# A retention layer and a two-step mixer on one core: the hand-written order of all work is searched anew

## The chip, the cores and the metric

The kernel runs on one core of a Trainium2 chip. Time is the device time of one execution in microseconds (us); lower is better. The kernel before takes 189.88 us, the median of three runs (189.71 to 190.01).

## The reference

For 4 batches, 8 heads, 768 positions and a head size of 64, a retention layer runs over the positions with a decaying state, and its result goes through a mixer that first mixes the 768 positions (through 256) and then the 512 channels (through 1536):

```python
gamma = 1.0 - 2.0 ** (-5.0 - np.arange(H))          # one decay per head
for t in range(S):                                   # retention
    state = gamma * state + k[:, :, t] (outer) v[:, :, t]
    y[:, :, t] = q[:, :, t] @ state / sqrt(D)
x = y, heads side by side: (4, 768, 512)
h  = relu(x.T @ w_tok1) @ w_tok2                     # 768 -> 256 -> 768
u  = x + h.T
out = u + relu(u @ w_ch1) @ w_ch2                    # 512 -> 1536 -> 512
```

## The kernel before

**Work.** There are 16 units for the first half, one for each batch (0 to 3) and pair of heads (0 to 3). A unit loads q, k and v of its two heads (768 positions in six chunks of 128). k is scaled by a decay (L343 on ACT, L345 on DVE) and transposed into `kT` (on PE, L379, and copied out of PSUM, L392; or by a DMA transpose on SP, L367). q is transposed into `qT` (PE, L377, then L387 on DVE with the decay; or L367). PE forms the state of each chunk (L408), DVE adds these up chunk by chunk (`U`, L418 and L420), and the sums are scaled into `diag` (L434 on ACT, L436 on DVE). PE forms the scores inside a chunk (L453), DVE masks them (`am`, L463), PE multiplies them with v (L474) and adds the part of the older chunks (L483). Then follow the two products of the position mixer (L503 with `wt1`, L523 with `wt2`) with a rectifier between (L512, L514), casts to 16 bits (L489, L529), a copy into `X` (L539) and a transpose into `uT` (PE, L568 and L575; or a DMA transpose on SP, L553).

The second half is done batch by batch: `widen` (512 to 1536 channels; L606 and L622 for batches 0 and 1, and a form with seven instead of eight products for batches 2 and 3, L647 to L717) and `narrow` (1536 to 512; L784 to L862, and L746 and L755 for the last five row blocks), with the stores to `out`.

**Loads.** Batches 0 and 1 are loaded by POOL with a cast to 16 bits (k, v and q of a pair are slabs of 192 KB each), between them the weights. k of the first pair, and all of batches 2 and 3, are requested by SP without a cast.

**The order.** Each piece of work is an `Op` with the engine it may run on. The string `PLAN` (L40) is the order in which all of them are written out, with the engine and the PSUM bank of each: two digits for an Op, one for the engine where it has a choice, one for each bank. Each engine executes its own instructions in the order in which they were written, and waits where an operand is not there. A `+` and a digit in `PLAN` stand for that many *zero products* (L935): products of a tile of zeros into bank 7 which nobody reads. The Ops' `deps`, costs and `dma` figures are what the search for `PLAN` works with; the program that is built depends on `PLAN` alone (`placed`, L70), and its waits follow from the tiles that are read and written.

Of the kernel before, what the change touches and what calls it, by code (L numbers as in the profile page):

```python
# [39 lines left out]
PLAN = (  # L40
    "0b04000a0903010d05020c060f1h11i107+h1j00e1W11k0081X0h+41l01m0g+81w011v230k1z+21n41A2x50i1y1o1p0j1S01T11q1r0m"
    "+91U31s1x1V00p+21Y42y1B226312706292t01Z2b2u020211t00l+9386221u02v1390n+11C1E51F1D0282z61G0230r2w02A2a2B0u241"
    "+72I102c42C2502L+11H31I2M2f12g1J02D2d2Q02E2e0+12H362h02K+11K2F01N2J1L02i62G11O00q2j2N31M11Q72k02O1P00E2l3412P0"
    "2o3512R0o2m01R13652p03710w2S03a72T62n03b2U0t3c2q03d3j452V03i123e0s3n2W3f4k62X03k3L70x3g03l2Z3h03m2r13003o23H1"
    "3p3r43103I13s2Y13253q03J03M3t03u33303v3K15s73w04l3N52s03x3A3y05taC10z3B0aF63C03z13D70y3F3E13V24303G1aD3OaG3Y0v"
    "bf7aE3XbgaHbc13P0Fbd4g14h1aL63Qbe3RaMbh0A4i43SaN3WaI14j00Dbl5bm0CaJ404bn4u2673aK0Bb353T04xbi13U03Z0Gbjb974P1bk"
    "4wba4304Q1444yb0641b44v4204R3b5b1451bb4T2b24m54V74S04n4614o474UbA6480b634pbB4qbJ24WbC4r494XbK4s1b74a1bL4cb8"
    "5326514b0aU3574d0aV1d4faR4aWaO15o14e055aP4t0aX34Y0I5p1aY4z60H4AaZaS56aQ0Kbu04ZaTbx30N504C1544D510bybM4B0bG7bv"
    "bObHbwbNbr24E0bs521bz4F019bIbo44G15bpbD7bqbE165q3602bQ45r04H118bS50MbFbt4I174L58259cc7bR15a0c84J05b35ccd14K0"
    "bX0bP5d0bVc94M04N05Y15e6cabW05f5Z0bZ5g162061cb5u6630651ch66c00bY0L675k5v68c44O5w5x5h5yc5c15i05z64bT5l0cj6ci1"  # L50
    "5m069cl5j0ck0Oc2cA2cm06acu6y05C10356z0cwcq5G6C00JcF45F6b05ncB5A0cy55D5B0cncr6B6D05E7806d7123cG5H0cz06ecJ6E790"
    "cv5I5K7cK5L5J0cD6f6A25M06h5N4cE05O6c10QcH6g5P00R7a05QcI10P5T5R0cx6i20W6j5U06l4co6m7b5V05S17f36F66k05W1cpce05X0"
    "6G6HcM6I6n06Jdn16Kdocfde66L1cQ07gcNcR1adF7cSdf7h7c0dq57idrdg7jdG7kds7d16o6dH6p7edz56q1dA7M16N6730dB7N10S6r6P7O"
    "cW56s06QcXdb76OcYdc6R7I0cZ3d0c37J06u6t06M1dR07Ldd6S51ed52dp6TcLd67K26U06V111dS1fd16Wd7dh76v17l0di6X1dO28S08T1"
    "6Y36w0dP8V6ZdTd24dQ701d80djcgd90V7m0bU716xcCda7n73267217P07qd3730740T7pcs0dk5d40U751dldC47Q7odmcT37RcU7rdDcV7S"
    "e671bdE77760e0e43e77X1465e1e508m0dX7e3dYe9818n1dw57Tea00Xdxe2dZ7s2a317ta20ed8k27U7Ydy0YdI07ZdJ12dU180dKdV8o8j1"
    "8i0dt61cdL0dW1gdM7V08l821dudN8U2eb4ee07u07v0dv7weO57x0eI7y6eJ7zeieL7A07W0eP7Bec7Ee883855ej8408p6eK86ef8708q8r"
    "7C0es38s7D0em8877F0eo898W07Heq2eg8X0eheT48a07G013et8ber0eU8YeM08c0en8d08e8tepeN0eX8f0eu8g0eR8u8heY8v08x45619w0"
    "eS18Z38A9x010ex7908w0c618zeV0Z918Bct1eveW0eycO1c7092f0cP18yew09y93ezf1949s1970415eA09508F399148GeE9t0f49608C4"
    "989v8DeB8E09b8H0f80eQ9c59a8I6f9a42eC8Jf59f19g8K0fm79u2eZ9d8L9e0eFfa6fnfceH1fb8M0fo29h08Of79i6fdfp9j8P1ff9k0fq"  # L60
    "eD8Rfg9z68N0a92f69ofraa9l8Q0aba5fe49A9m0acfkfh9n0ftfs39Bfuf21adfiae9p0fD5fv9q0fy9Cgm2fE9DfF1fz9EfHfjflfwfGfI"
    "9H4076gnfxfR1a609JfKfSfJ3fAfLfT09KfV9F0fMfP9G0fUgqfWga79LfNa70fYfOgrgo6a8g80fCgpgtg9ge3fBfZfX6gbfQgc9Ig3gugs5"
    "gAgdgyg4gvgfgz9P1g09Qgggwg6g1ghgkg59M29NglgBgi9O0h34gZ9R0g29S0af09Tgjh40gH6gx9U0h19Vah5037h09W09Yag0g7alh89Z0"
    "gCa00ha7a1ak9X0ajgJ1ek0gDh90gI09rap0aih52gEaqam5h2hch6anhbgMao0gGhd0hegKar0h7eG0hhgLgN1as1hlatgFgQau0el0hfhp1"
    "hmgR0hgavhq0gO7aw0hnax0ayhihr2hoaz0gPaA0huaBhshtgVhv0hk0hj1gSgWgY1hw2gThHhL6hygUhxig7hz0hJi10hMhZ4hIihhAhKhN5"
    "hBhPhCii3hQikhOhDhF1ilf31i0hR5hEgX0hSijhG1inhTi3ioim3hUi4iL1ipi52i6i2hVhXi7hWiu0ibi8iZ5idici9ieiviqiahYiw4iyir"
    "j0iN6ixiMisizj3iPj4j14iBj2j6iCiR3iOiQiA4jdj7iGiDiSitj56iHiJjY7iTj8iEifjbiUj9jciXjek60jaiYk7jZiIjCk0k1jEk2iFiV"
    "iKk8iWk9kak3jfjDjk3jFkbjl0jG4jgk4jI1jH0jijN6k51jLjOjhjr7jM0kcjRjjjJjPjsjSjpjKjQ0jTjUjq0jtjW1jVkd1jX0jvju0ke4jw"
    "jm6jxjyjnjA1kfjokgkhjzkikjjB0kkkl0"
)  # L70


# [24 lines left out]
def kernel(  # L97
# [171 lines left out]
    def load(b, p, what):  # L269
        src = dict(k=k, q=q, v=v)[what][b, 2 * p:2 * p + 2]  # L270
        hard = (b, p, what) in HARD
        plain = b in PLAIN
        wide = what == "q" and TURN[b, p, "q"] == "w"
        inner = what == "k" and not hard and not plain
        s = Slot("us" if hard else "v" if what == "v" and not plain else "row")
        if inner:
            s = pairs[b, p]

        def emit():
            if plain:  # L280
                t = tile_of(s, [P, 2, NC, D], FP)
                nc.sync.dma_start(out=t, in_=src.rearrange("h (c p) d -> p h c d", p=P))
                return
            if hard:
                t = tile_of(s, [P, 3, N2], FP)
                t = s.tile = t.rearrange("p a b -> p (a b)").rearrange("p (h c d) -> p h c d", h=2, c=NC)
            elif what == "v":
                t = tile_of(s, [P, 2, NC, D], F16)
            else:
                t = (s.tile if inner else tile_of(s, [P, 2, 2, NC, D], F16))[:, int(inner)]  # L290
            if wide:
                nc.gpsimd.dma_start(out=t.rearrange("p h c d -> p h (c d)"),
                                    in_=src.rearrange("h (p c) d -> p h (c d)", c=NC))
            else:
                (nc.sync if hard else nc.gpsimd).dma_start(out=t, in_=src.rearrange("h (c p) d -> p h c d", p=P))
# [672 lines left out]
```

## Time and profile before

| | |
|---|---|
| median of 3 runs | 189.88 us (189.71 to 190.01) |
| the profiled execution | 189.72 us |
| its span, from the first to the last instruction | 187.9 us |
| PE busy | 182.2 us (97%) |
| DVE busy | 163.0 us (87%) |
| ACT busy | 126.2 us (67%) |
| zero products (L935) | 62, busy 14.8 us |

PE, DVE, ACT, POOL and SP are the engines; PEld is the weight load of PE. A row such as `L935 PE MATMUL bank<-zero ... x62 | 14.8, 382` names the line, the engine, the operation, its tiles, how many there are, the time in which at least one of them was running, and the mean duration of one in ns. Products overlap on PE, so that the busy time divided by the count is less than the mean. Between 189.72 us and the span lie 1.8 us outside the first and the last instruction.

### The profile page before, as it was taken

What the parts mean: (1) busy time and instruction counts of PE and PEld (TensorE: products, weight loads), DVE (VectorE), ACT (ScalarE), POOL (GpSimd) and SP (SyncE); (2) the same over time, 40 slices, a digit from 0 to 9 for tenths busy, and PEclk for the clock granted to TensorE, in tenths of its full rate; (3) what the DMA queues carried; (4) which work ended last, traced back from release to release, by engine and by line L of the source; (5) the groups of instructions that cost most, each with busy time, mean ns of one, the idle gap of its engine ahead of it and who ended that gap; (6) DMA issues with size and microseconds to landing.
All of it is one profiled execution on the core that took longest, in us unless ns stands there. A gap on an engine that the chain in (4) does not pass through costs nothing.

```text
span 187.9 us, 5270 instructions
## 1 busy us (share of the span) xinstructions
PE 182.2 (97%) x2102; PEld 137.5 (73%) x2102; DVE 163.0 (87%) x424; ACT 126.2 (67%) x288; POOL 36.2 (19%) x45
## 2 busy tenths in 40 slices
PE   7999999999999999999999999999999999999993
PEld 3556789667679879767677988875589986656882
DVE  3789899978799998989896999999999988879973
ACT  7227789677868697579868696899975535682220
POOL 8992659520020001000103100210000000000000
PEclk9999999999999999999999999999999999999999
DMA  6999999999999799999999999998206464500133
GB/s 101 168 165 196 175 178 187 172 187 207 187 211 221 153 116 222 193 203 205 194 244 161 220 149 221 349 161 214 42 0 108 147 65 176 197 0 5 56 140 140
DMA packets 94233, 30.23 MB, mean 161 GB/s; under 512 B 84352, under 2 KB 91264, under 8 KB 94208
## 3 DMA queue, kind: packets, MB, share of 16 engines
q1 hardware_dynamic: 62560, 18.95, 56.1%
q0 software_dynamic: 30208, 8.46, 44.0%
q10 hardware_dynamic: 1440, 2.49, 4.5%
q8 instruction: 16, 0.26, 0.6%
q14 instruction: 9, 0.07, 0.2%
HBM read 26.74 MB, written 6.29 MB: 176 GB/s over the span
## 4 chain that ended last, share of the span: by engine, by line
PE 82%; DMA 5%; ACT 5%; DVE 4%; issue 1%; DVEq 0%; ACTq 0%
PE bank L606 14%; PE bank L820 13%; PE bank L679 12%; PE bank L830 9%; PE bank L935 6%; PE bank L523 6%; PE bank L503 6%; PE bank L453 3%; PE bank L474 3%; DMA qT<-q 3%; PE bank L746 3%; DMA uT<-u 2%; PE bank L483 2%; PE bank L408 2%; PE bank L377 2%; ACT h L622 2%
## 5 line engine op out<-in xcount | busy, mean ns | idle before, releaser
L463 DVE TENSOR_TENSOR am<-bank,mask 128x384 f16<-128x384 f32 x64 | 33.6, 549 | 4.4 <-PE bank L453 4.0
L606 PE MATMUL bank<-uT,wc 128*128 128x384 f16 x192 | 36.0, 326 | 0.0
L622 ACT ACTIVATE h<-bank 128x384 f16<-128x384 f32 x48 | 21.6, 491 | 9.1 <-PE bank L606 7.2
L606 PEld LDWEIGHTS <-wc 128*128 128x128 f16 x192 | 17.4, 98 | 9.1 <-DVE uT L575 0.2
L360 POOL CAST v<-row 128x768 f16<-128x768 f32 x7 | 7.4, 1067 | 76.6 <-DMA row<-in_v_dram 50.4
L696 DVE TENSOR_TENSOR h<-bank,us 128x384 f16<-128x384 f32 x36 | 18.9, 552 | 2.8 <-PE bank L679 1.8
L810 ACT COPY us<-bank 128x256 f32<-128x256 f32 x27 | 10.1, 377 | 15.8 <-PE bank L820 15.6
L820 PEld LDWEIGHTS <-hs 128*128 128x128 f16 x198 | 18.7, 98 | 2.4
L837 DVE TENSOR_TENSOR X<-X,bank 128x256 f32<-128x256 f32 x44 | 17.7, 414 | 2.4 <-PE bank L830 1.5
L691 ACT COPY us<-bank 128x384 f32<-128x384 f32 x36 | 16.3, 490 | 4.3 <-PE bank L679 3.3
L489 ACT CAST x<-bank 128x384 f16<-128x384 f32 x30 | 14.0, 487 | 6.7 <-PE bank L483 6.6
L420 DVE SCALAR_TENSOR_TENSOR U<-U,gp,bank 128x64 f32<-128x64 f32 x64 | 17.4, 275 | 1.0
L820 PE MATMUL bank<-wsum,hs 128*128 128x256 f16 x132 | 17.6, 273 | 0.0
L935 PE MATMUL bank<-zero 128*128 128x384 f16 x62 | 14.8, 382 | 1.1 <-DVE zero L928 1.1
L679 PE MATMUL bank<-hs,wsum 128*128 128x384 f16 x72 | 15.0, 326 | 0.1
L529 ACT CAST u<-bank 128x384 f16<-128x384 f32 x27 | 12.6, 487 | 3.5 <-PE bank L523 3.3
L523 PE MATMUL bank<-h,wt 128*128 128x128 f16 x192 | 14.8, 219 | 0.0
L434 ACT ACTIVATE diag<-U,gp 64x320 f16<-64x320 f32 x25 | 13.8, 558 | 0.4
L679 PEld LDWEIGHTS <-wsum 128*128 128x128 f16 x96 | 9.3, 97 | 6.4 <-issue 0.5
L503 PE MATMUL bank<-x,wt 128*128 128x128 f16 x192 | 13.7, 219 | 0.0
L830 PEld LDWEIGHTS <-h 128*128 128x128 f16 x132 | 12.5, 98 | 1.5
L539 ACT COPY X<-bank 128x384 f32<-128x384 f32 x28 | 13.4, 494 | 0.1
(89 smaller groups left out, 365.8 us busy)
## 6 DMA issues: line engine op xcount, KB each, us to landing
out_dram<-X SPq DMA_DIRECT2D x14, 256.0 KB, 4.3
row<-in_v_dram SPq DMA_DIRECT2D x8, 384.0 KB, 5.5
row<-in_k_dram SPq DMA_DIRECT2D x8, 384.0 KB, 6.0
row<-in_q_dram SPq DMA_DIRECT2D x8, 384.0 KB, 5.5
wc<-in_moe_w_ch_dram POOLq DMA_DIRECT2D x5, 512.0 KB, 12.6
out_dram<-X ACTq DMA_DIRECT2D x9, 256.0 KB, 3.0
row<-in_q_dram POOLq DMA_DIRECT2D x8, 192.0 KB, 6.1
v<-in_v_dram POOLq DMA_DIRECT2D x8, 192.0 KB, 8.4
```

Source lines behind the costliest of these rows:

```text
L420: nc.vector.scalar_tensor_tensor(out=u[:, c], in0=u[:, c - 1], scalar=gp[:, p:p + 1], in1=st, op0=ALU.mult, op1=ALU.add)
L463: nc.vector.tensor_tensor(am, SC[g].tile[:, :m * P].rearrange("p (i t) -> p i t", t=P), mask.to_broadcast([P, m, P]), ALU.mult)
L503: nc.tensor.matmul(acc[:, jt * P:(jt + 1) * P], wt1[:, i, jt * P:(jt + 1) * P], X16.tile[:, i], start=(i + jt == 0), stop=(i == NC - 1), s ...
L523: nc.tensor.matmul(Y[hf].tile[:, i * P:(i + 1) * P], wt2[:, jt, t], H1.tile[:, jt], start=False, stop=(jt == NJ - 1), skip_group_check=True)
L606: nc.tensor.matmul(acc[:, :SH], wc1[:, ct, ft * P:(ft + 1) * P], UT.tile[:, ct, sh * SH:(sh + 1) * SH], start=(ct == 0), stop=(ct == NP - 1))
L622: nc.scalar.activation(H2.tile[:, ft], A.tile[:, :SH], AF.Relu)
L679: nc.tensor.matmul(acc[:, :SH], left(ct), r[:, ct], start=first and ct == 0, stop=ct == 1, skip_group_check=True)
L696: nc.vector.tensor_tensor(into(hf)[:, ft], bank.tile[:, :SH], kept(j), ALU.add)
L820: nc.tensor.matmul(acc_[:, lo], l[:, j], r[:, j], start=first and j == 0, stop=j == K2 - 1, skip_group_check=True)
L830: nc.tensor.matmul(acc_[:, lo], l[:, j], r[:, j], start=first and j == 0, stop=j == K2 - 1, skip_group_check=True)
L837: (nc.vector if e == "DVE" else nc.gpsimd).tensor_tensor(dst(), dst(), b_(), ALU.add)
L935: nc.tensor.matmul(spare[:, :384], zero[:, :P], zero, start=True, stop=True)
```

## The change

`PLAN` is replaced as a whole; the Ops, their instructions and the data they move are the same. In the search's rules one condition is dropped: a request for k no longer waits for the landing of q of the same pair, which shares its tile.

```diff
 PLAN = (
-    "0b04000a0903010d05020c060f1h11i107+h1j00e1W11k0081X0h+41l01m0g+81w011v230k1z+21n41A2x50i1y1o1p0j1S01T11q1r0m"
...
+    "00010b04050703021h0080f061i1+e1n00d1o1p1j11k00a1q1r1s1t0090e1u00c0g+11l2+21W01m0h1X0i0j+11v210k1w341z1S11A0m1x"
...
         elif inner:
-            o = Op(ops, (-20, 0, b, p), [("POOL", 1000, 1000, emit)], [loads[b, p, "q"][2]], [], [s], dma=dma,
+            o = Op(ops, (-20, 0, b, p), [("POOL", 1000, 1000, emit)], [], [], [s], dma=dma,
                    after=queue[-6:-5], behind=queue[-1] if queue else None)
```

Zero products: 62 before (17 ahead of the first product with data, 45 later), 32 now (14 ahead, 18 later, in groups of 1 to 5). No instruction of another kind is added or removed on PE. Between ACT and DVE some pieces change places: DVE has three instructions fewer, ACT two more and one store of SP's, and POOL casts one more v (8 instead of 7).

The first place is the opening of POOL's queue. `row` is a tile that takes q and then k of a pair, `v` one that takes v, `wt1` the first weight. Before:

```order
L212 IOTA us_87 128x384
L192 IOTA away_66 128x128
L292 DMA row_90<-in_q_dram 128x2x384
L292 DMA row_104<-in_q_dram 128x2x384
L292 DMA row_116<-in_q_dram 128x2x384
L295 DMA v_122<-in_v_dram 128x12x64
L295 DMA row_90<-in_k_dram 128x12x64
L295 DMA v_179<-in_v_dram 128x12x64
L295 DMA row_116<-in_k_dram 128x12x64
L292 DMA row_225<-in_q_dram 128x2x384
L295 DMA v_257<-in_v_dram 128x12x64
L257 DMA wt1_78<-in_moe_w_tok1_dram 128x6x256
```

Of the change:

```order
L192 IOTA away_66 128x128
L212 IOTA us_98 128x384
L295 DMA v_122<-in_v_dram 128x12x64
L292 DMA row_155<-in_q_dram 128x2x384
L292 DMA row_169<-in_q_dram 128x2x384
L295 DMA row_169<-in_k_dram 128x12x64
L292 DMA row_178<-in_q_dram 128x2x384
L295 DMA row_178<-in_k_dram 128x12x64
L295 DMA v_212<-in_v_dram 128x12x64
L295 DMA v_216<-in_v_dram 128x12x64
L257 DMA wt1_78<-in_moe_w_tok1_dram 128x6x256
L292 DMA row_228<-in_q_dram 128x2x384
```

v of the first pair (`v_122`) is now requested first instead of fourth; k of the second pair moves from fifth to fourth, and `wt1` from tenth to ninth.

The second place is DVE behind its small constants. `k16` is the scaled k, `U` the running state, `am` the masked scores, `qT` the transposed q. Before:

```order
L233 MEMSET diag_77 128x960
L387 TENSOR_TENSOR qT_177<-bank1_161,gq_72 128x768
L387 TENSOR_TENSOR qT_198<-bank0_185,gq_72 128x768
L463 TENSOR_TENSOR am_227<-bank0_209,mask_75 128x384
L463 TENSOR_TENSOR am_242<-bank1_210,mask_75 128x384
L463 TENSOR_TENSOR am_259<-bank3_218,mask_75 128x384
L418 COPY U_261<-bank4_231 128x64
L420 SCALAR_TENSOR_TENSOR U_261<-U_261,gp_73,bank4_231 128x64
L345 TENSOR_SCALAR k16_265<-row_90,gk_69 128x6x64
L420 SCALAR_TENSOR_TENSOR U_261<-U_261,gp_73,bank4_231 128x64 x3
L463 TENSOR_TENSOR am_288<-bank2_217,mask_75 128x384
L387 TENSOR_TENSOR qT_307<-bank5_244,gq_72 128x768
```

Of the change:

```order
L345 TENSOR_SCALAR k16_119<-us_96,gk_69 128x6x64
L418 COPY U_157<-bank0_144 128x64
L420 SCALAR_TENSOR_TENSOR U_157<-U_157,gp_73,bank0_144 128x64 x4
L234 TENSOR_SCALAR mask_75<-away_66 128x128
L387 TENSOR_TENSOR qT_210<-bank2_182,gq_72 128x768
L387 TENSOR_TENSOR qT_214<-bank0_197,gq_72 128x768
L463 TENSOR_TENSOR am_238<-bank3_230,mask_75 128x384
L345 TENSOR_SCALAR k16_240<-row_169,gk_69 128x6x64
L463 TENSOR_TENSOR am_242<-bank4_231,mask_75 128x384
L463 TENSOR_TENSOR am_245<-bank2_220,mask_75 128x384
L463 TENSOR_TENSOR am_274<-bank1_221,mask_75 128x384
L463 TENSOR_TENSOR am_284<-bank3_266,mask_75 128x384
```

The five steps of the first pair's state (`U_157`), which need `v_122`, now stand ahead of the first `qT`; k of the second pair is scaled one place behind the first `am`.

The third place is SP's queue where the transposes of the last batch's `uT` stand between stores. Before:

```order
L367 DMA_TRANSPOSE qT_2849<-q16_2805 128x6x128
L553 DMA_TRANSPOSE uT_2683<-u16_2987 128x6x128
L553 DMA_TRANSPOSE uT_2683<-u16_2735 128x6x128
L553 DMA_TRANSPOSE uT_2683<-u16_3152 128x6x128
L862 DMA out_0_dram<-X_1881 128x512
L862 DMA out_0_dram<-X_1881 128x512
```

Of the change:

```order
L367 DMA_TRANSPOSE qT_2952<-q16_2807 128x6x128
L862 DMA out_0_dram<-X_1110 128x512
L553 DMA_TRANSPOSE uT_2800<-u16_2696 128x6x128
L862 DMA out_0_dram<-X_1110 128x512
L553 DMA_TRANSPOSE uT_2800<-u16_2943 128x6x128
L862 DMA out_0_dram<-X_1829 128x512
L553 DMA_TRANSPOSE uT_2800<-u16_3152 128x6x128
L862 DMA out_0_dram<-X_1110 128x512
```

A store now stands ahead of each of the three requests.

More of the change, by code (lines that the diff above doesn't have):

```diff
@@ L46 @@
[L46 to L65, printed above, removed]
@@ new lines @@
+    "1T0+51U31V0+427321y26142a0l0n292x02y2t01E5+11Y41Z2021281F1B3222u02v62w01C1D00p0q0r0u2z02b2A232I612B2M0E+32H24"
+    "2C2D2E2J1G0+11H11I2c02402502d2K2F02e02G02f22g1J12L384392h12N12Q60t1K1L01M11N1O00o2i42j2R2k03413512O2P02S01Q3"
+    "1P11R12l0x2m02n03643a50s0w3713b3c2o2p02q00v2T32U2V03d3e3j403i722r33f3m3g03h02W2X02Z0z3L44k53k3003103n2Y03l3r0"
+    "3o23p3s3263H13I13q03t03J13K02s13u33v0A4l3w03303N55s73x3y03z03M3A3B03V64315taI73Y0y3D23E03W3F3G10F3O3X3Z3PaC33Q"
+    "aF63R3C1aL20Cbf4bc1bdaDbebgaEbhaM4g0bJ0bKbL4h13S0D3T1aNaGb05b1b2aJaKbl4aH4i04j1b92bmbnbabb4u60754w3U04m44T3bA2"
@@ new lines @@
+    "4ybB40541b304U0BbD14P14Q04x433444nb44v420467450bEb51dbC47bF4804R0bx2by494c4o4p4q4S1530716bz4a14r5o04V254b6457"
+    "5p04s1b74WaX0aY4X4z6554b0b80G4t04d14Y4Z4faO4aPaQ0I4e1aR5aSaTaU7aV4AaZ0H5q550bo3aW4B04C24D4E0bi7511bM5r0bN56bP"
+    "5804F44Gbj6020O7a2bG15214H04I1e4L17br459bsbp5b54J04K15c4M04N0bQ25a0bqbH5d0bk5e35fcc7bObI0M151618btbu4bv0KbS1bT"
+    "5g05h5Y14ObwbX45Z161bYc8c9bR05i0bVbW05k5u15v653665w0N5l05m0675x685ycd1bZc005zca6y06z0c1c26215j0c4c563064chci0"
+    "5C01560Lcj469cuclckcy26a5E5Dcv0R0J5A0cz0cncA05H15B07805G790cD5FcB5I0P5ncE0cocbcm06d05636h6e5K4cH6B6C15L5J05M0"
@@ new lines @@
+    "dX5dY7x07y07z7A0dZ8oe51e9ea0820dJdK1ccLcO0eb5853ed7B8S012e38s8t8u8U2eIeK838408Y867C07E7D0ec8708T1cpe61efeJ7F0"
+    "8827G0eLee0898a0ege7e89s0eT7eUeiem8b8c1eO2eP9t08eejeM1enep8d08VeX8f0eoeY119v8x6025es4eN0eR8B8AeteS08v08h8z8w0"
+    "0Zeq5eV8y1b970427eher0c617H9a8Z69091928g0cs0eW014ev988C38D9w0f0eQ93f1949x0ex2ey8F08Gew0ez8E08H08I1eZeA095099"
+    "a21a309bf48J8K0f5fm6eEeF960f84eu8Lf9fn9c79d9e08M0f78N09f19geB9h0fcfdek18O9i39jel0fqa429k0eCa5eDf68P08Q0fa2fbfr"
+    "a93aaab9z59Aac9lfffo2fD09B9m09n0fp9ofgfe7fh9p09q0ft9C9D9Efkf31fF2fEfu9yfs1fvfHfyflfIadfGfifzfjfwfxfK9H26459K"
@@ new lines @@
+    "fR7fLfPfJ1fS9Jaeg849F09G0fQ9Igm6gnfX3fM8R9LfVfWa61fT2fUa70fNfOfAgqgrg9go5gpg5fYgs2fZga1gcg0gtg3ge5gbgAgdgfgugv"
+    "gy9M19Ng1ggfBgzgkghgwgBgxg49P79Qg6gigj9O0gH69S2glgZ9R09T9U0h35h19Yh40h09V9W09X0h8a8g2g7gCgI0ah3240ha1h90fChc"
+    "9Z0ajgDhbeH1gJ2heaf0ag0gFalgEh2gO0aihfa00gMhd1am3anao0akh519rh6h7hheG1ap4aqgKgN0as1a1gQar0atau0gGhlhp2gPgSavhg"
+    "hj1hnhq0gR0gVhihw5hmgWayhoaw0az0aA0aBgThr6hxhuhv0hAhshthygLhHhL6gUhz0f21hBhCig4hDhEhIhMhZ5i10ii1ihhN2i0i3i4hP"
+    "hJim7ikhQi6hSax0ilhR3inhOiji2i7ibhKhThUiw0ioi51ipi8hXhVhWichYiqiriZ5j0iL6iu3i9iaivixiIj3iN7iyj4jY1iMiOizj6iP"
@@ L70 @@
+    "iA0iQifj17j2iBiCj7jdgY1j52iSgX1iR7j8iDiTiGiHisitiUjeiXjbjck63j9hk0iViYidiEiJiejCjZjEjDk0iWk7iFjG6jN5jH0jaiKjf"
+    "jgk1k2hF1jLjhjijk2jOjl1k8jM0jPjFk3jQ0jRk4k50jr0jsjpjI1jjjSjJhG0jKjq0jtjTjUju0jW0jVjX0jvk9kakbjwjxjm6kcjnkd1jy"
+    "ke3kfjokgjzjA0khkijB1kjkkkl0"
 )
```

13 lines of the change are left out of this document (5 added, 8 removed).

## Prediction

> **What bounds the kernel now.** I read the page's busy times first.
>
> ```profile
> PE 182.2 (97%) x2102; PEld 137.5 (73%) x2102; DVE 163.0 (87%) x424; ACT 126.2 (67%) x288; POOL 36.2 (19%) x45
> L935 PE MATMUL bank<-zero 128*128 128x384 f16 x62 | 14.8, 382 | 1.1 <-DVE zero L928 1.1
> ```
>
> PE is never free, but 14.8 of its 182.2 us are zero products. Where they lie is told by the table of stages, for everything and then for L935 alone (columns: the stage, its length, then busy time and count of PE, PEld, DVE, ACT, POOL).
>
> ```profile
> 6.70:22.60 15.90, 15.74 (x234) 10.31 (x232) 13.30 (x33) 7.61 (x14) 11.44 (x14) 1.00 1.93 175
> 22.60:33.00 10.40, 10.40 (x212) 9.44 (x210) 10.03 (x24) 9.70 (x23) 7.60 (x9) 1.00 1.78 184
> 33.00:184.70 151.70, 150.54 (x1646) 115.06 (x1644) 136.19 (x338) 104.77 (x245) 11.10 (x12) 1.00 0.94 160
> 184.70:188.00 3.30, 0.00 (x0) 0.00 (x0) 0.41 (x1) 0.00 (x0) 0.00 (x0) 0.94 0.37 135
> ...
> 6.70:22.60 15.90, 9.23 (x46) 3.87 (x45) 1.00 1.93 175
> ```
>
> All zeros end by 22.6 us. From there PE works without a gap to 184.7, and 3.3 us of last addition and store follow. So the kernel has two parts: an opening in which PE waits for others (with zeros in the waits), and 162 us of PE work that no other order can shorten unless it removes waits. These are what the waits of PE itself come to:
>
> ```profile
> PE bank L453 <- DMA qT<-q: 0.6, 1, 0.6
> PE bank L679 <- DMA uT<-u: 0.2, 1, 0.2
> PE bank L408 <- ACT h L622: 0.2, 1, 0.2
> ```
>
> That is 1.0 us. The change must win in the opening: how much earlier does PE reach its unbroken work? Four milestones of PE mark the opening.
>
> ```profile
> 10.14 0.51 PE L453 MATMUL bank<-qT,kT 64*128 64x128 f16 x12
> 14.61 0.51 PE L453 MATMUL bank<-qT,kT 64*128 64x128 f16 x12
> 20.41 0.83 PE L503 MATMUL bank<-x,wt 128*128 128x128 f16 x12
> 22.42 0.83 PE L523 MATMUL bank<-h,wt 128*128 128x128 f16 x12
> 32.82 0.65 PE L606 MATMUL bank<-uT,wc 128*128 128x384 f16 x3
> ```
>
> **The zeros that go.** The first block and a later one:
>
> ```profile
> 1.13 5.62 PE L935 MATMUL bank<-zero 128*128 128x384 f16 x17 [1.13 <-DVE zero L928]
> 8.73 1.47 PE L935 MATMUL bank<-zero 128*128 128x384 f16 x8
> ```
>
> One costs 5.62/17 = 0.33 us in the first block and 1.47/8 = 0.18 later. Three fewer ahead and 27 fewer later free 1.0 + 4.9 = 5.9 us of PE. That is no gain by itself: what stands behind a zero is waiting for a load or for DVE. So I follow these.
>
> **Landings.** Issues from the timeline, and the time from issue to landing of the first of each from the table of DMA issues, taken at that moment:
>
> ```profile
> 1.46 2.28 POOL L292 DMA_DIRECT2D row<-in_q_dram  x3
> row<-in_q_dram POOLq DMA_DIRECT2D x1, 192.0 KB, 4.6
> ...
> 3.73 1.03 POOL L295 DMA_DIRECT2D v<-in_v_dram  x1
> v<-in_v_dram POOLq DMA_DIRECT2D x1, 192.0 KB, 6.3
> ...
> 4.75 1.15 POOL L295 DMA_DIRECT2D row<-in_k_dram  x1
> row<-in_k_dram POOLq DMA_DIRECT2D x1, 192.0 KB, 6.7
> ...
> 9.60 1.56 POOL L257 DMA_DIRECT2D wt<-in_moe_w_tok_dram  x2
> wt<-in_moe_w_tok_dram POOLq DMA_DIRECT2D x1, 384.0 KB, 8.2
> wt<-in_moe_w_tok_dram POOLq DMA_DIRECT2D x1, 384.0 KB, 9.7
> ...
> 21.06 0.80 POOL L257 DMA_DIRECT2D wc<-in_moe_w_ch_dram  x1
> wc<-in_moe_w_ch_dram POOLq DMA_DIRECT2D x1, 256.0 KB, 8.4
> ```
>
> q lands at 6.1, v as the fourth slab at 10.0, k at 11.4, `wt1` at 17.8, `wt2` (issued at 10.4) at 20.1, the first `wc1` at 29.5: about 1.3 us a slab at first, 1.07 later. In the changed order v is first. Its landing there is not shown: not before 6.1 (q's, at that place), nor after 1.46 + 6.3 = 7.8. I take 6.6: q's 6.1, 0.3 for the longer issue (1.03 against 2.28/3), 0.2 for the slower slab; it is nearest to that row. Then q at 7.7, q 8.9, k 10.2. `wt1` has one slab less ahead: 17.0. `wt2` is eleventh as before: 20.1 to 20.3. The first `wc1` also has the same slabs ahead: 29.5. So dropping the hold on k moves few bytes earlier. The request of k did not wait for q on the chip either: 4.75 lies ahead of q's landing at 6.1. The change is the order alone.
>
> **DVE behind these.** Its groups from 6.7 to 33 us (count, busy time, mean ns):
>
> ```profile
> L463 DVE TENSOR_TENSOR am<-bank,mask 128x384 f16<-128x384 f32 x16 | 8.3, 548 | 1.3 <-PE bank L453 1.3
> L387 DVE TENSOR_TENSOR qT<-bank,gq 128x768 f16<-128x768 f16 x7 | 6.6, 949 | 1.0 <-PE bank L377 1.0
> L420 DVE SCALAR_TENSOR_TENSOR U<-U,gp,bank 128x64 f32<-128x64 f32 x16 | 4.4, 275 | 0.3
> L345 DVE TENSOR_SCALAR k<-row,gk 128x384 f16<-128x384 f16 x5 | 1.8, 386 | 0.0
> L392 DVE COPY kT<-bank 128x768 f16<-128x768 f16 x2 | 1.1, 550 | 0.2 <-PE bank L379 0.2
> L418 DVE COPY U<-bank 128x64 f32<-128x64 f32 x4 | 0.9, 214 | 0.0
> ```
>
> and of ACT, in the same stretch:
>
> ```profile
> L489 ACT CAST x<-bank 128x384 f16<-128x384 f32 x8 | 3.6, 496 | 1.4 <-PE bank L483 1.4
> L392 ACT COPY kT<-bank 128x768 f16<-128x768 f16 x3 | 2.4, 805 | 3.6 <-PE bank L379 3.6
> ```
>
> L408 can start at 6.6 and takes 0.35 with its tail. DVE's five steps of `U_157` (0.2 + 4 x 0.3) run from 7.0 to 8.4, the mask to 8.6; the first `qT` ends at 9.6, so the first L453 stands at 9.75 (10.14 before). The second `qT` ends at 10.5, an `am` follows, the scaled k ends at 11.2; transpose 0.5, copy 0.8 on ACT, and the second pair's L453 stands at 12.8 instead of 14.61. From `am_284` at 13.2 DVE has no break up to `qT_776`, which the last L453 ahead of L606 needs: 12 `am` x 0.52, 4 `qT` x 0.94, 12 steps x 0.275 and 3 copies x 0.22 of `U`, 4 k x 0.36, 6 copies of 0.55 and a rectifier of 0.35 (by columns, from `am`) are 19.1 us. Such sums are too long: the rows above come to 23.1, the four smaller groups of that table to 3.7, together 26.8, where DVE was busy 13.30 + 10.03 = 23.3 in the two stages. Unlike neighbours overlap by 13%. So 16.6, and `qT_776` ends at 29.8; `am_454`, 19 instructions behind `am_284`, ends at 20.4.
>
> **PE behind DVE.** Behind the second L453 stand eight short groups of PE, 2.7 us with the third pair's transpose; its `kT` (0.8) and two casts (0.45 each, overlapping) bring ACT to 17.1. L503 needs these and `wt1` (17.0), and the last four zeros stand ahead: 17.9, instead of 20.41. The first L523 needs `wt2` (20.2) and stands behind the L474 that needs `am_454` (20.4): 20.8 instead of 22.42. From there to the first L606 both orders hold the same products, and the change one L453 more (0.5): 10.4 + 0.5, so 31.7. `qT_776` (29.8) and `wc1` (29.5) are there by then. L606 is 1.1 us earlier with 0.5 us more work behind it: **1.6 us gained**, of 5.9 freed. The rest of the zeros' time becomes plain waiting.
>
> **What follows.** Two of PE's waits behind 33 us change. The rows are from the chain of waits:
>
> ```profile
> 65.24 5.28 DMA qT<-q
> ...
> 146.84 0.66 PE bank L820 x6
> ...
> 150.47 0.33 PE bank L523 x6
> 151.34 4.36 DMA uT<-u
> ```
>
> The `qT` of batch 2 that held PE 0.6 us: its q is now SP's fifth load instead of its third, but its casts are split between ACT and DVE, and only one load stands between its transpose and kT's; I count half of the wait as gone, -0.3 (bounds -0.6 and +0.8). The last `uT`: L523 ends at 150.80, the transpose lands at 155.70, 4.9 us later, and the products that PE has in between (six groups of L820 and L830 at 0.66 and three of L679 at 0.32, two products of 384 columns as two late zeros) come to 4.9 too, hence the small wait of 0.2. In the change there are five of 0.66 and three of 0.32, 4.2: **+0.7** (bounds 0 and +1.5: a store of `X_1829` that waits for DVE is now ahead of this request). The last products, addition and store are of the same kinds as before: 3.3 us stay. The pieces that change between DVE, ACT and POOL cost nothing as long as L606 keeps PE busy (ACT is at 105 of 152 us there); without this cover each is about 0.5.
>
> Sum: -1.6 - 0.3 + 0.7 = -1.2 us on the execution of 189.72, so 188.5. The runs' median lies 0.16 above the profiled execution: **188.7 us**.
>
> **Rivals.** *DVE does not hold PE in the opening* (chance 0.21): if PE's order, not DVE's, sets the pace, L606 comes when `wc1` lands, 29.5 to 30, and 3 to 3.3 us are won: 186.2 to 187.5. For it: DVE idled 2.6 us of 15.9 in the stage to 22.6. Against it: 10.03 of 10.40 in the next.
>
> *PE's slow start lasts longer* (0.15). Zeros take 0.33 up to 6.7 us and 0.18 from there: PE's speed doubled after 5.6 us of unbroken products. Now the stream breaks after 14 x 0.32 = 4.5 us, for 1 us, until v lands. If the count starts anew, PE is slow to 12.2; the transposes, L408, L453 and nine zeros up to there are 3.6 us of fast time, which doubled fill the stretch and push the second pair back by 0.75 to 1.6 us: 189.5 to 190.2, no change. (The Trainium skill, "TensorE: Matmul & The Clock Gate", Part 1, puts it as a free-running window of 3.4 us that must be busy. By that rule the gate would open one window after 6.7, at 10.1, and the loss would be the smaller of the two. The trace agrees that the first 3 us were not enough; no run here shows a broken stream.)
>
> *DVE's opening is held by v, and the kernel is slower* (0.19). The five `U` steps stand ahead of the first `qT`, so DVE can do nothing until the first slab is there, and everything up to `qT_776` is one queue. If v lands at 7.8, all of it moves by 1.2 us; if the overlap of 13% is only half there in that queue, `am_454`, and with it L523, moves by another 0.5. Those 1.7 us are more than the 1.2 gained in all, and the kernel ends near 190.4. It decides from 1.6 us of delay on. For it: the fourth slab's 6.3 us, and that this order lets DVE rest nowhere. Against it: that slab had three ahead of it.
>
> **Numbers.** The forecast has 0.45 (187.9 to 189.5), the three rivals 0.21, 0.15 and 0.19. A difference under 0.2%, 0.4 us, cannot be told from none here. Faster: 0.66; the same: 0.15; slower: 0.19. The range takes half of the first rival and most of the last: 186.8 to 190.6; the forecast's own is 187.9 to 189.5.
>
> **What would show it.** Right: first L453 of the first two pairs near 9.8 and 12.8; the first L523 near 20.8; the first L606 near 31.7 with DVE unbroken from 13 us; waits of PE for others in the opening that were zeros before; a wait for `uT` near 152 of about 0.9. Wrong: L606 at 30 or at 33; L408 later than 7.5; products at 0.32 per 384 columns behind 7 us; a wait over 1 us behind 33 that is neither of the two.

## The result, and the profile after

The changed kernel takes **191.59 us** (median of four runs, 191.34 to 191.70) against 189.80 us for the kernel before, timed beside it; the forecast was 188.7 us. The ratio is 1.0101, 95% interval 1.0069 to 1.0133: it is **slower by 1.0%**, 1.9 us by the ratio. Ratios leave out executions in a slower state of the chip and the medians do not, so that the two need not agree exactly. Timed again later beside other kernels (`changed_again`), it gave 1.0106 (1.0073 to 1.0138).

The opening kept close to the times that were forecast. The timeline of TensorE (PE) of the changed kernel (start, duration, what, and the idle time ahead with what ended it):

```profile
6.08 0.35 PE L408 MATMUL bank<-v,k 128*64 128x64 f16 x10 [0.84 <-DMA v<-in_v_dram]
9.01 0.51 PE L453 MATMUL bank<-qT,kT 64*128 64x128 f16 x12
12.10 0.51 PE L453 MATMUL bank<-qT,kT 64*128 64x128 f16 x12 [0.24 <-ACT kT L392]
17.38 0.83 PE L503 MATMUL bank<-x,wt 128*128 128x128 f16 x12 [0.16 <-DVE am L463]
20.21 0.84 PE L523 MATMUL bank<-h,wt 128*128 128x128 f16 x12
31.23 0.66 PE L606 MATMUL bank<-uT,wc 128*128 128x384 f16 x3
32.62 0.33 PE L568 MATMUL bank<-ident,u 128*128 128x128 f16 x3 [0.57 <-ACT uT L575]
```

The first L606 stands at 31.23 us instead of 32.82, with 0.5 us more work done; 0.57 us go back at once, waiting for `uT`. So about 1.5 us are won by 33 us. They are lost again, and more. PE's waits of 0.3 us and over behind 30 us (total, count, longest):

```profile
PE bank L503 <- ACT X L539: 1.2, 1, 1.2
PE bank L453 <- DMA qT<-q: 1.1, 1, 1.1
PE bank L606 <- ACT h L622: 0.7, 1, 0.7
PE bank L568 <- ACT uT L575: 0.6, 1, 0.6
PE bank L474 <- DVE am L463: 0.4, 1, 0.4
PE bank L820 <- DVE us L810: 0.3, 1, 0.3
```

Before there were three, of 0.6, 0.2 and 0.2. The table of stages tells where. First the kernel before, for 78 to 110 us (length, busy time and count of PE, PEld, DVE, ACT, POOL; then PE's granted clock, the share of the 16 DMA engines, which is above 1 here, and GB/s):

```profile
78.00:110.00 32.00, 31.84 (x356) 23.77 (x354) 28.43 (x72) 24.03 (x56) 3.39 (x3) 1.00 1.26 202
```

And the changed kernel:

```profile
78.00:110.00 32.00, 28.99 (x327) 21.23 (x324) 26.06 (x64) 23.42 (x56) 2.96 (x4) 1.00 1.15 208
```

From 78 to 110 us PE is idle 3.01 us instead of 0.16. The DMA share is above 1 in both kernels: the rows of batches 2 and 3 are requested from about 50 to 120 us. The chain of waits goes through them. Its share by engine, where the kernel before had 82% PE and 5% DMA, and some of its pieces:

```profile
PE 54%; DVE 20%; DMA 15%; ACT 5%; SPq 3%; issue 2%; POOL 0%; ACTq 0%; DVEq 0%; POOLq 0%
...
77.08 5.18 DMA qT<-q
...
87.73 5.58 DMA row<-in_q_dram
93.42 1.12 ACT q L343 x2
...
99.49 6.60 DMA row<-in_k_dram
```

Three places of the timeline, all engines, show how a late delivery reaches PE:

```profile
82.39 0.32 PE L453 MATMUL bank<-qT,kT 64*128 64x128 f16 x5 [1.12 <-DMA qT<-q]
...
93.42 1.12 ACT L343 ACTIVATE q<-row,gy 128x384 f16<-128x384 f32 x2 [0.80 <-DMA row<-in_q_dram]
94.97 0.32 PE L606 MATMUL bank<-uT,wc 128*128 128x384 f16 x1 [0.68 <-ACT h L622]
...
106.11 0.61 ACT L343 ACTIVATE k<-row,gk 128x384 f16<-128x384 f32 x1 [2.63 <-DMA row<-in_k_dram]
107.91 0.49 PE L503 MATMUL bank<-x,wt 128*128 128x128 f16 x6 [1.21 <-ACT X L539]
```

At 82 us the transpose itself is late. At 94 and 107 us the row is not what PE needs: ACT has its scaling (L343) next in its queue, stands still until the row lands, and the `h` and the `X` that PE needs stand behind it. In the kernel before neither ACT nor DVE waits 0.2 us or more for a row between 34 and 130 us. In the profile of `changed_again` the same three waits of PE are 0.8, 1.7 and 0.3 us: the places and the sum stay, the single sizes do not.

Waits are not the whole loss. From the first L606 to the end of PE's last product the table of stages has, before and after:

```profile
32.82:184.65 151.83, 150.72 (x1649) 115.17 (x1646) 136.36 (x337) 104.95 (x245) 11.28 (x12) 1.00 0.94 160
31.23:186.61 155.38, 150.99 (x1638) 115.08 (x1634) 138.78 (x334) 103.78 (x245) 11.54 (x13) 1.00 0.91 158
```

PE starts this stretch 1.6 us earlier, is idle in it 4.4 us instead of 1.1, and busy 0.3 us longer: together the 2.0 us by which the spans differ. It is busy longer although an L453 (twelve products, 0.45 us) now stands ahead of the stretch, so the same products take PE some 0.7 us more in the new order. The profiles of `no_stores` and `all_cures`, which come below, show the same (151.04 and 150.84 us for these products). Why is open.

### The profile page after: what moved, and what is told of

Its sections match the earlier page's. It is cut to its first block, busy times and chain, and to the rows that moved or that the text cites. A ratio compares the mean times of both kernels' runs of the same rounds, so it can differ in the third digit from the quotient of the medians.

```text
span 189.9 us, 5212 instructions
## 1 busy us (share of the span) xinstructions
PE 178.6 (94%) x2072; PEld 134.9 (71%) x2072; DVE 165.8 (87%) x421; ACT 126.7 (67%) x290; POOL 35.9 (19%) x46
## 4 chain that ended last, share of the span: by engine, by line
PE 54%; DVE 20%; DMA 15%; ACT 5%; SPq 3%; issue 2%; POOL 0%; ACTq 0%; DVEq 0%; POOLq 0%
PE bank L679 14%; PE bank L820 8%; PE bank L830 7%; PE bank L606 6%; DMA row<-in_q_dram 5%; DVE am L463 4%; DMA row<-in_k_dram 3%; PE bank L523 3%; PE bank L503 3%; PE bank L746 3%; DMA qT<-q 3%; DMA v<-in_v_dram 2%; DVE wsum L904 2%; DVE U L420 2%; DVE hs L784 2%
## 5 line engine op out<-in xcount | busy, mean ns | idle before, releaser
L606 PE MATMUL bank<-uT,wc 128*128 128x384 f16 x192 | 36.4, 326 | 0.8 <-ACT h L622 0.7
L606 PEld LDWEIGHTS <-wc 128*128 128x128 f16 x192 | 17.3, 98 | 10.0 <-issue 1.1
L810 ACT COPY us<-bank 128x256 f32<-128x256 f32 x29 | 10.6, 377 | 15.2 <-PE bank L820 12.2
L837 DVE TENSOR_TENSOR X<-X,bank 128x256 f32<-128x256 f32 x44 | 17.9, 415 | 1.5 <-PE bank L830 1.0
L529 ACT CAST u<-bank 128x384 f16<-128x384 f32 x29 | 13.7, 484 | 4.4 <-PE bank L523 4.1
L503 PE MATMUL bank<-x,wt 128*128 128x128 f16 x192 | 13.9, 219 | 1.4 <-ACT X L539 1.2
L523 PE MATMUL bank<-h,wt 128*128 128x128 f16 x192 | 15.0, 219 | 0.0
L503 PEld LDWEIGHTS <-wt 128*128 128x128 f16 x192 | 12.0, 98 | 2.6 <-issue 1.8
L523 PEld LDWEIGHTS <-wt 128*128 128x128 f16 x192 | 12.3, 98 | 1.5
## 6 DMA issues: line engine op xcount, KB each, us to landing
v<-in_v_dram POOLq DMA_DIRECT2D x8, 192.0 KB, 10.2
```

The source lines that it names most:

```text
L503: nc.tensor.matmul(acc[:, jt * P:(jt + 1) * P], wt1[:, i, jt * P:(jt + 1) * P], X16.tile[:, i], start=(i + jt == 0), stop=(i == NC - 1), s ...
L523: nc.tensor.matmul(Y[hf].tile[:, i * P:(i + 1) * P], wt2[:, jt, t], H1.tile[:, jt], start=False, stop=(jt == NJ - 1), skip_group_check=True)
L606: nc.tensor.matmul(acc[:, :SH], wc1[:, ct, ft * P:(ft + 1) * P], UT.tile[:, ct, sh * SH:(sh + 1) * SH], start=(ct == 0), stop=(ct == NP - 1))
L837: (nc.vector if e == "DVE" else nc.gpsimd).tensor_tensor(dst(), dst(), b_(), ALU.add)
```

## The experiments

Most kernels here join pieces of the two orders, or move a few steps of one. In the diffs `new` and `old` are the steps of the two `PLAN`s, and a step already written out is not written again. A table at the end gives all ratios against the kernel before.

**Where the loss lies: the two halves apart.** `new_open`, called the fast kernel below, is the new order up to the first L606, the old one behind; `old_open` is the mirror.

```diff
-PLAN = new
+PLAN = new[:200] + [s for s in old if s not in new[:200]]    # new_open; 4 steps differ at the seam
+PLAN = old[:200] + [s for s in new if s not in old[:200]]    # old_open
```

> The new order up to the place of the first L606 (about 31 us), with its 32 zero products, and behind it the old order. Theory A (the loss lies in the order behind 40 us, where TensorE's waits rose from 3.73 us to 7.19 us between the two profiles; the opening itself gained about 1.5 us): 189.8 less 1.5, about 188.3 us, with the three waits of the changed kernel at 81, 94 and 106 us gone. Theory B (the loads of batches 2 and 3 come at the pace of their queue and their four buffers, so an earlier start is only waited away): about 189.7 us, with new waits on loads behind 60 us. Theory C (fewer zero products leave TensorE slower for the rest): about 191.4 us.

> The mirror: the old order with its 62 zero products up to the place of the first L606 (about 33 us), and behind it the new order. Theory A: the changed kernel's 191.6 us and the 1.5 us that the opening gains there, about 193.1 us, with the waits at 81, 94 and 106 us as large as in the changed kernel. Theory B: the products reach those places 1.5 us later, so the waits there shrink by it and the time stays at about 191.6 us. Theory C: about 189.8 us.

`new_open` takes 188.39 us, ratio 0.9932 (0.9909 to 0.9956), what theory A gave. B and C fall for it: the loads of the old order were asked for 0.4 to 3.2 us earlier too, and the 32 zero products did not cost time. Its row for 78 to 110 us:

```profile
78.00:110.00 32.00, 31.84 (x366) 24.31 (x364) 28.98 (x72) 25.61 (x61) 3.63 (x3) 1.00 1.09 194
```

`old_open` takes 195.45 us, 1.0300 (1.0265 to 1.0335), more than any theory gave. Its waits include one of 1.4 us for `X` at the seam and one of 1.7 us for `hs` (L647) that neither parent has, so its size can't be put down to the new order alone. Its direction is A's.

**The first result again, and the seam moved.** `fast_again` is `new_open` once more; `new_to_38` has the seam 40 steps later.

> The new order up to 31 us and the old behind it, once more: 188.4 us if the first result stands; above 189.3 us if it was chance, as the cut at 38 us suggests.

> The new order up to some 38 us and the old behind it, to see how far the gain reaches and whether 31 to 38 us shares in the loss. Theory F (the deliveries of batches 2 and 3, asked for from 50 us on, carry the loss): 188.4 us, as with the cut at 31 us.

`fast_again`: 188.66 us, 0.9963 (0.9941 to 0.9984). The gain stands, at 0.7 to 1.3 us. `new_to_38`: 189.56 us, 1.0023 (0.9993 to 1.0052), against the expectation. Its timeline has, beside the new order's own wait for `uT`, two that stand in neither parent:

```profile
37.34 0.51 PE L379 MATMUL bank<-ident,k 128*128 128x128 f16 x6 [0.52 <-ACT k L343]
...
39.17 0.34 PE L474 MATMUL bank<-v,am 128*128 128x64 f16 x6 [0.50 <-ACT kT L392]
```

A seam has a price, some 1 us here.

**Is it the zero products?**

```diff
 # zero products in the kernel before, group by group
-17, 4, 8, 2, 9, 2, 9, 1, 7, 1, 1, 1
+17, 1, 2, 1, 3, 1, 3, 1, 1, 1, 1
```

> The kernel before with 32 zero products instead of 62 (17 ahead of the first real product as before, then 1, 2, 1, 3, 1, 3, 1, 1, 1, 1 where it has 4, 8, 2, 9, 2, 9, 1, 7, 1, 1, 1), its order untouched. By the prediction's step (a) and its term for DVE the products taken out leave waits of the same length: 189.6 us, unchanged within 0.3. If the zero products held real work up: 188.7 us. If fewer of them leave TensorE's clock lower for longer: above 190 us.

(Step (a) is the prediction's part on the zeros that go.) 189.34 us, 1.0002 (0.9979 to 1.0024): the time is unchanged, as that part had it, but not for its reason. PE reaches the first L606 2.0 us earlier than in the kernel before (32.82), behind the same products, and waits that away later:

```profile
30.86 1.14 PE L606 MATMUL bank<-uT,wc 128*128 128x384 f16 x6
...
79.01 0.61 ACT L343 ACTIVATE q<-row,gy 128x384 f16<-128x384 f32 x1 [1.07 <-DMA row<-in_q_dram]
80.06 0.83 PE L503 MATMUL bank<-x,wt 128*128 128x128 f16 x12 [1.06 <-ACT h L622]
...
129.42 0.51 PE L453 MATMUL bank<-qT,kT 64*128 64x128 f16 x12 [1.58 <-DMA kT<-k]
```

PE's waits in the opening come to 3.3 us, the 30 zeros taken out to 5.4 at the prediction's 0.18 each, so some zeros had held real work up. How much of the 2.0 us is theirs is open, since the first 17 zeros, the same in both, took 4.29 us here and 5.62 us there. At 79 us ACT stands still for a row, and the `h` that PE needs stands behind it, as in the changed kernel.

**Single waits cured in the changed kernel.** `casts_later` (ACT's queue; on DVE the other half of k goes behind one addition) and `qt_first` (SP's queue):

```diff
-L343 ACTIVATE q x2
+L343 ACTIVATE q
 L622 ACTIVATE h x2
+L343 ACTIVATE q
...
-L343 ACTIVATE k
 L489 CAST x
 L529 CAST u
 L539 COPY X
 L489 CAST x
+L343 ACTIVATE k
```

```diff
 L367 DMA_TRANSPOSE kT
+L367 DMA_TRANSPOSE qT
 L862 DMA out_dram<-X
 L282 DMA row<-in_k_dram
-L367 DMA_TRANSPOSE qT
```

> The changed kernel with two scalings of late loads put behind the evictions that queued behind them: on ScalarE q (L343, at 93.4 us) behind the next two h, and k (L343, at 106.1 us) behind the next X and x, and its other half on VectorE behind one addition to X. Theory A, with strict queues as the cause: the waits of TensorE at 93.96 us (0.85 us) and 106.43 us (1.37 us) go but for some 0.2 us, so 191.6 less 2.0, about 189.6 us. Theory B: the waits move to the next product that needs a load; about 191.4 us.

> The changed kernel with one transposition moved up on SyncE's queue: qT of the second pair of batch 2 (L367, issued at 77.08 us) ahead of the store of X (L862) and the load of k (L282) that stand before it. Theory A: it is issued and lands 1.1 us earlier, the wait of TensorE at 80.94 us falls from 1.28 us to about 0.2 us, and nothing takes its place: about 190.5 us. Theory B: the load and store that are now later, and the loads behind them, make the waits at 94 and 106 us longer by as much: about 191.5 us.

191.68 us, 1.0089 (1.0056 to 1.0122), and 191.53 us, 1.0094 (1.0060 to 1.0128): each within the error of the changed kernel's 1.0101. The waits aimed at are gone from their profiles. (In that of `casts_later` the row of q also landed 1.3 us earlier, at 92.0 us, so ACT's wait for it, and PE's at 94 us, might have gone without the move. The eleven times of `casts_later` lie in two groups, five from 190.46 to 190.96 us and six from 191.68 to 192.64; the profile is of the first.) Of `casts_later`, PE's longest behind 30 us:

```profile
PE bank L453 <- DMA qT<-q: 1.0, 1, 1.0
PE bank L453 <- DMA kT<-k: 0.6, 1, 0.6
```

and of `qt_first`, in which the wait for `qT` is gone, and a second wait for `h`, one for `hs` and one for `v` stand there instead:

```profile
PE bank L606 <- ACT h L622: 1.4, 2, 0.8
PE bank L679 <- DVE hs L647: 0.6, 1, 0.6
...
PE bank L408 <- POOL v L360: 0.5, 1, 0.5
```

Theory A in the form "each wait at its full price" falls for the three waits: behind the first L606 PE is idle 3.7 us in the profile of `casts_later` and 4.5 us in that of `qt_first`, against 4.4 in the changed kernel's. What it gains at one wait, it largely waits at another.

**Stretches exchanged.**

> The new order up to some 64 us, the old order behind it. Theory D (the loss lies between 64 and 123 us, where the loads of batches 2 and 3 come in, and is one loop of loads, scalings and transpositions rather than single waits, since the two single cures returned nothing): about 188.5 us, as with the old order from 31 us on. If the loss is prepared earlier, by the order in which the first loads of batch 2 are asked for (50 to 64 us): 190 us or more.

> The new order up to 31 us, the old order from there to about 123 us, the new order behind. Theory D: about 188.5 us, since the part behind 123 us holds no load of a row and lost nothing in the changed kernel's profile (0.6 us of waits against 0.9). If the part behind 123 us shares in the loss: up to 190 us.

191.75 us, 1.0118 (1.0097 to 1.0140), and 193.65 us, 1.0197 (1.0169 to 1.0224): neither as theory D had it, though the first lies where its rival did (190 us or more). From 78 to 110 us, where both have the old order, the loss is gone; PE's busy time there in `new_to_64`:

```profile
78.00:110.00 32.00, 31.85 (x368) 23.81 (x367) 28.67 (x73) 23.75 (x56) 2.84 (x3) 1.00 1.07 193
```

But near the seams stand waits of 1.4 us for `us` (65 us) and, in the profile of `old_mid`, which is of an execution of 196.17 us, of 3.9 us for a cast on ACT (121.7 us). These two say nothing on theory D beyond that; seams in the middle of full queues can't be read here for their parts.

**The stores.** The new order issues four stores of batch 0 (256 KB each) between 75.9 and 103.1 us, among the loads; the old one issues its own from 114.7 us on (but one). `stores_late` moves the four back, `no_stores` leaves them out, `early_stores` brings them forward in the fast kernel.

```diff
 # stores_late: SP, then ACT
-L862 at 75.9, 98.7 us        +L862 x2 behind the store at 117.7 us
-L862 at 98.0, 103.1 us       +L862 x2 behind the store that follows on ACT
 # no_stores: the four are not issued
 # early_stores: new_open with these four at the new order's places and engines, 94.6 to 100.5 us
```

> The changed kernel with the four stores of batch 0 that it issues at 75.9, 98.0, 98.7 and 103.1 us (L862) put back behind the store at 117.7 us, where the old order has them. Theory E (the early stores hold SyncE's queue and share the DMA engines with the loads: the load of k issued at 99.49 us took 6.6 us to land beside them): the loads behind them land 0.6 to 2 us earlier, and the time falls by 1 to 1.5 us, to about 190.3 us. Theory D: about 191.4 us.

> The changed kernel without the four stores of batch 0 that it issues between 75.9 and 103.1 us (that part of the output is not written); nothing else is moved. Theory F (from 30 to 130 us the 16 DMA engines are busy throughout, so each transfer put among them pushes back all behind it; the four stores are 1 MB, 5 us at the 205 GB/s of that stretch): the loads and transpositions behind 76 us land up to 1.5 us earlier each, the waits of TensorE at 94 and 107 us shrink, and the time falls to 189.5 to 190.3 us. If only the order in the queues of the engines counts: 191.3 us.

> The reverse on the fast kernel (new order up to 31 us, old order behind, 188.4 us): its four late stores of batch 0 (112.6 to 116.3 us) issued at some 90 to 103 us instead, on the engines and in the places that the new order gives them, as far as the additions ahead of them allow. Theory F with the stores as the main part: loads behind 92 us land 1 to 3 us later, 189.5 to 190.5 us. If the stores are not the main part: 188.0 to 188.6 us.

`stores_late` takes 196.43 us, 1.0357 (1.0319 to 1.0395). The waits at 94 and 107 us are gone, but ACT stands still for 4.8 us ahead of a copy that PE needs. Two of the moved stores are issued in that time; the profile names the landing of a row of v as what ended the wait. The last row is of the table of stages:

```profile
117.38 2.83 ACTq L862 DMA_DIRECT2D out_dram<-X  x2
120.24 0.37 ACT L810 COPY us<-bank 128x256 f32<-128x256 f32 x1 [4.83 <-DMA row<-in_v_dram]
120.67 0.59 PE L820 MATMUL bank<-wc,hs 128*128 128x256 f16 x2 [4.24 <-ACT us L810]
...
120.67:124.00 3.33, 3.33 (x22) 2.56 (x22) 1.19 (x4) 1.73 (x4) 0.15 (x1) 0.50 1.10 239
```

Behind PE's stop its granted clock is 0.50 for the next 3.3 us, so part of this kernel's time is the clock. What held the stores up to 117.38 us is open. `no_stores` is easier to read: 190.71 us, 1.0050 (1.0020 to 1.0080), 0.5% or 1.0 us less than the changed kernel, with intervals that overlap a little. It prices the four stores as such and not their place alone, since it issues them nowhere else. The row of k at 106 us lands 1.1 us earlier (its lines are one lower):

```profile
105.00 0.61 ACT L342 ACTIVATE k<-row,gk 128x384 f16<-128x384 f32 x1 [1.49 <-DMA row<-in_k_dram]
```

`early_stores` shows the same from the other side, with the place alone changed: 190.47 us, 1.0053 (1.0019 to 1.0087), 1.7 to 2.3 us more than the fast kernel's 0.9963 and 0.9932. The three loads of q from 88 to 112 us, median from issue to landing, in the fast kernel:

```profile
row<-in_q_dram SPq DMA_DIRECT2D x3, 384.0 KB, 5.3
```

and with the stores among them:

```profile
row<-in_q_dram SPq DMA_DIRECT2D x3, 384.0 KB, 7.2
```

That stores among the loads are a part of the loss is shown from both sides; its size, 1.0 us of 1.9 by `no_stores`, is less sure.

**The order of the loads.** Is the rest in the order in which rows are asked for, scaled and transposed? `new_loads` puts that part of the new order into the fast kernel, `old_loads` that part of the old order into the changed kernel, `old_loads_stores` the stores too.

```diff
 # L282, L343/L345, L357 to L360 and L367 of batches 2 and 3
-PLAN = base
+PLAN = [s for s in base if s not in loads], with the loads' steps of the other order
+       set in where PE's work has come as far as it had there
```

> The fast kernel with one part of the new order alone: the loads of rows, their scalings, the conversions of v and the transpositions of q and k of batches 2 and 3 (L282, L343/L345, L357 to L360, L367) stand in the new order and on the engines that it gives them, everything else in the old. If the order of these deliveries carries the loss: about 191.5 us. If not: 188.4 us.

> The changed kernel with one part put back: loads of rows, their scalings, the conversions of v and the transpositions of q and k of batches 2 and 3 stand in the old order and on the old engines, at the same progress of TensorE's work; everything else, the four early stores too, in the new order (one product L408 and two additions to U of the first pair of batch 3 are put behind the later k that they read). Theory F (the order of deliveries on busy DMA engines carries most of the loss, the early stores some 1 us): about 189.3 us. If the order of the other engines carries it: 191.3 us.

> As the one before, with the stores (L862) too in the old order. Theory F: about 188.4 us, as with the whole old order from 31 us on. If the order of the other engines carries the loss: 190.3 us or more, the changed kernel less what its early stores cost.

`new_loads`: 194.79 us, 1.0209 (1.0145 to 1.0272). `old_loads`: 191.43 us, 1.0101 (1.0067 to 1.0134). `old_loads_stores`: 191.69 us, 1.0135 (1.0087 to 1.0183). So this part of the new order is slow in the old surroundings, and the old one no better in the new. In `old_loads` the three waits are gone or small (0.2 us for `qT`), and others are there, among them:

```profile
PE bank L820 <- DVE us L810: 1.0, 1, 1.0
PE bank L820 <- ACT us L810: 0.9, 2, 0.6
```

Theory F, that the order of deliveries by itself carries most of the loss, falls. That it is the fit of the deliveries and the queues that use them is what these runs suggest; they do not show it, since seams have a price of their own.

**The last wait of the fast kernel.**

```diff
 # SP, new_open
+L367 DMA_TRANSPOSE kT
 L367 DMA_TRANSPOSE qT
 L282 DMA row<-in_q_dram
-L367 DMA_TRANSPOSE kT
```

> The fast kernel with kT of the third pair of batch 3 ahead of qT of the same pair and of the last load of q on SyncE's queue, and the two scalings of its k moved up on ScalarE and VectorE. Its profile shows the transposition issued at 119.77 us and landed 8.7 us later, and TensorE waiting 1.37 us for it at 126.98 us, the only wait above 0.6 us behind 20 us. Theory F (deliveries are the bound there and their order decides): it lands by 126 us, 187.2 us. If qT or the last q, now later, takes its place: 188.0 to 188.4 us.

188.78 us, 0.9955 (0.9922 to 0.9987): the wait is gone, the time the same within the error. In the profile of `fast_again`, the same program as `new_open`, the wait does not stand either, with the same span. One profile's wait need not be in the next.

**The three cures together,** the deciding run: the moves of `casts_later`, qT ahead of one load as in `qt_first`, and no early stores.

> The changed kernel with three cures together: the scalings of casts_later, qT ahead of the load of k as in qt_first, and the four early stores left out as in no_stores (that part of the output is not written). If the waits at 81, 94 and 106 us are costs of their own that only uncover one another: 188.9 us (the 191.5 less the 2.6 us that they held in the changed kernel's second profile beyond what the fast kernel waits there). If the remaining order makes new waits in their place: 190.6 us, as with the stores left out alone.

189.74 us, **1.0016** (0.9992 to 1.0039): as the kernel before, 0.85% or 1.6 us below the changed kernel's 1.0101, and between the two expectations. PE's waits behind 30 us, and its row for 78 to 110 us:

```profile
PE bank L678 <- DVE hs L646: 0.6, 1, 0.6
PE bank L567 <- ACT uT L574: 0.6, 1, 0.6
PE bank L819 <- DVE us L809: 0.3, 1, 0.3
PE bank L452 <- DMA qT<-q: 0.3, 1, 0.3
```

```profile
78.00:110.00 32.00, 31.55 (x355) 23.64 (x353) 27.42 (x69) 24.88 (x60) 3.47 (x4) 1.00 1.17 198
```

Idle there: 0.45 us instead of 3.01. Together the cures return 1.6 us, well beyond the error. The stores alone are 1.0 of it; whether the two others add the remaining 0.6 is not shown, since the intervals of `all_cures` and `no_stores` overlap and neither of the two moved the time by itself.

| kernel | ratio | 95% interval | PE idle, 78 to 110 us |
|---|---|---|---|
| changed, twice | 1.0101, 1.0106 | 1.0069 to 1.0138 | 3.0, 2.9 |
| new_open, twice | 0.9932, 0.9963 | 0.9909 to 0.9984 | 0.2, 0.2 |
| kt_first | 0.9955 | 0.9922 to 0.9987 | 0.2 |
| new_to_38 | 1.0023 | 0.9993 to 1.0052 | 0.3 |
| few_zeros | 1.0002 | 0.9979 to 1.0024 | 1.2 |
| casts_later | 1.0089 | 1.0056 to 1.0122 | 1.4 |
| qt_first | 1.0094 | 1.0060 to 1.0128 | 2.0 |
| no_stores | 1.0050 | 1.0020 to 1.0080 | 1.3 |
| all_cures | 1.0016 | 0.9992 to 1.0039 | 0.5 |
| early_stores | 1.0053 | 1.0019 to 1.0087 | 0.9 |
| old_loads | 1.0101 | 1.0067 to 1.0134 | 1.7 |
| old_loads_stores | 1.0135 | 1.0087 to 1.0183 | 1.5 |
| new_loads | 1.0209 | 1.0145 to 1.0272 | 2.8 |
| new_to_64 | 1.0118 | 1.0097 to 1.0140 | 0.2 |
| old_mid | 1.0197 | 1.0169 to 1.0224 | 0.2 |
| old_open | 1.0300 | 1.0265 to 1.0335 | 1.8 |
| stores_late | 1.0357 | 1.0319 to 1.0395 | 0.4 |

The last column is of one profile each. `few_zeros`, as fast as the kernel before, has 1.2 us where that has 0.16, so a difference under 1 us in it means little.

`new_open` beats both kernels: the new order for the first 31 us, the old for the rest.

## Why the prediction was wrong

**The zeros: right in the time, not in the reason.** Thirty fewer leave the time as it was (`few_zeros`). The prediction's reason was that "what stands behind a zero is waiting for a load or for DVE". In the one profile PE came to the first L606 2.0 us earlier without them and lost that behind 78 us. That the time did not move was luck.

**Landings: right in their order, the first ones 0.4 to 0.7 us early.** v was there at 6.04 us, not 6.6, the two q's behind it at 7.1 and 8.2 (7.7 and 8.9), k at 9.8 (10.2), `wt1` at 16.5 (17.0); `wt2` (20.1) and `wc1` (29.5) as forecast. The steps that hang on the first are earlier by about as much: the L453s at 9.01 and 12.10 (forecast 9.75 and 12.8), L503 at 17.38 (17.9), L523 at 20.21 (20.8).

**The opening's gain: right in size; its cause is open.** L606 stands at 31.23 (31.7) and 1.5 us are won by 33 us (1.6 forecast). But `few_zeros` is there as early with none of the new order's moves, so that v and DVE's order made the gain is not shown. `new_open` was faster than the kernel before by 0.7 to 1.3 us. `few_zeros`, with the same order behind the opening and the first L606 at the same moment (30.86 and 30.91 us), was not: an earlier L606 alone decides nothing. The one wait that the step did not have is `uT`'s 0.57 us at 32.6 us: half of that copy is on ACT in the new order.

**"What follows": wrong; this step failed.** It said that two of PE's waits behind 33 us change. The wait of 0.6 us for the first `qT` of batch 2 went altogether, more than the half counted; the last `uT`, forecast at +0.7, cost nothing; both were inside their bounds. But three others came, at 82, 94 and 107 us, with 3.0 us in all; two of them are over 1 us, the sign of an error that the text itself named. The sentence that let them pass is "The pieces that change between DVE, ACT and POOL cost nothing as long as L606 keeps PE busy". It counted the pieces and summed ACT's busy time (105 of 152 us), and did not ask of each scaling of a row whether its row has landed when the queue comes to it. ACT has time to spare; here it spent some of it standing still ahead of something that PE needed. The four stores that the new order moves forward to 76 to 103 us, on SP and ACT, have no term in the prediction at all: `no_stores` puts 1.0 us on them, in a stretch with a DMA share of 1.15. What the sum lacked: +2.9 us of idle PE from 78 to 110 us, of which the three cures returned 1.6 in time, and the 0.7 us that the same products took longer behind the first L606; the sum had taken their time as unchanged.

**The rivals.** The slower one had the right direction (190.4 us) for a reason that did not occur: v was early, and DVE was not held by it. Of the first, L606 at 29.5 to 30 did not occur; but its premise, that PE's own order sets the pace of the old opening, fits `few_zeros` better than the forecast's does. Nor did the slow start occur: behind the break ahead of L408 the products ran at full speed, L408's ten in 0.35 us. That rival had a page's rule beside it. The Trainium skill ("TensorE: Matmul & The Clock Gate", Part 1) has the window run free, so that the switch comes at another moment in each execution. The runs agree: the 14 first zeros of one and the same program took 3.76 us in the profile of `new_open` and 4.41 in that of `fast_again`, and the spans were 186.7 and 186.6 us.

**What stays open.** Between `all_cures` (1.0016) and `new_open` (0.9932 and 0.9963) 0.5 to 0.8%, 1.0 to 1.6 us, are not assigned. Waits are only a part: behind the first L606 PE is idle 2.1 us in the profile of `all_cures`, and 1.9 and 1.4 in the two of `new_open`. Its busy time is another: 150.84 us with an L453 (0.45 us) less work, against 150.59 and 150.97. It is open, too, why the row of q requested at about 88 us lands after 4.1 us in the profile of `casts_later` and after 5.0 to 5.9 in five others of the new order.
